# K and V in 256 KB transfers into rings freed per two heads, with at most 1.3 MB in flight

## The chip, the cores and the metric

One Trainium2 chip, one of its cores. The metric is the device time of one execution in microseconds (us), as a median of several runs. Traces were taken by the hardware profiler on one execution of each kernel. The engines are called by their names in the profile: PE is TensorE (PEld its weight loads), DVE VectorE, ACT ScalarE, POOL GpSimd, and SP SyncE, whose queue issues the loads. The granted clock is the share of full clock speed that PE was allowed; at half clock it is one half.

One run of the kernel before, 1038.62 us, was slow and is not compared. Kernels that were run only once, with a profile, have the state "unknown" and are used for their mechanism, not for their time to a per cent. The profiled execution of the kernel before took 1035.58 us, 1% more than its median.

## The reference

Two independent attention blocks, A and B, with a cached K and V; their outputs are concatenated.

```python
# B=16, Sq=64, D=640, H=32, Sk=512, Dh=128, all bfloat16; twice (A and B)
q      = (x @ wq).reshape(B, Sq, H, Dh).transpose(0, 2, 1, 3)
scores = einsum("bhqd,bhkd->bhqk", q, k_cache) * Dh**-0.5
p      = softmax(scores)
o      = einsum("bhqk,bhkd->bhqd", p, v_cache)
y      = o.transpose(0, 2, 1, 3).reshape(B, Sq, H*Dh) @ wo
```

K and V of both blocks are 268 MB; with the weights, and x once for each half of the heads, the kernels here read 294.65 MB.

## The kernel before

A static plan. For every pair of batches and every pair of heads, one *step* runs: PE transposes K (32 small matmuls), projects q (10), makes scores (4), transposes the probabilities (16), multiplies by V (16) and by wo (4). There are 256 steps. PE's whole program is unrolled, about 42,000 matmuls and weight loads.

All loads go through SP's queue, in an order that the plan fixes. K and V come in pieces of G heads of one batch:

```python
class Cfg:
    G = 4               # heads in one K or V transfer: 4 * 512 * 128 * 2 bytes = 512 KB
    NKB = 5; NVB = 5    # ring slots, each of G heads of two batches
    NXN = 1             # one buffer for x
    ...

# build_plan: the loads, with the step from which the slot is free and the step that needs it
    for c in range(NCHUNK):
        ...
        for kind, ring, n_ring, cons, tb in (("LDK", "kn", cfg.NKB, "KX", 2), ("LDV", "v", cfg.NVB, "PV", 2.5)):
            ready = NEG if c < n_ring else MPC * (c - n_ring + 1) - 1 - OFF[cons]
            need = MPC * c - OFF[cons]
            ...                                     # two transfers, one for each batch
# SP issues in order of need; a transfer waits only for the readers of its slot:
        op.deps = [d for d in deps if d is not op and not (d.eng == op.eng and op.eng in ("pe", "sp"))
                   and not (d.dma and op.dma and d.eng == op.eng)]
# the emitter
            src = blocks[blk][1][2 * bp + j, h0 + hlo:h0 + hhi].rearrange("(hp hs) (p t) d -> (hs p) hp t d", hs=2, t=8)
            ins = e.dma_start(kn_ring[:, c % NKB, j, hlo // 2:hhi // 2], src)
```

So the only limit on the bytes in flight is that a ring slot must be free.

Of the kernel before, what the change touches and what calls it, by code (L numbers as in the profile page):

```python
# [19 lines left out]


class Cfg:
    G = 4
    HH = 16
    NKB = 5
    NVB = 5
    NX = 3
    NXN = 1
    NQ = 2
# [24 lines left out]
        act=("EX0", "EX1", "XE0", "OE0", "OVP0", "ST0"),  # L54
        pool=("NM0", "NM1"),
    )
    TAIL_SPLIT = 2
    SLOT_NS = 3040.0
    DMA_NS = dict(LDK=1340.0, LDV=1460.0, LDWQ=1800.0, LDWO=1900.0, LDX=700.0)


class Op:
# [16 lines left out]
        self.dma = kind in DMA_KINDS  # L79


def build_plan(dims, cfg, stable):
    NBLK, B, H = dims["NBLK"], dims["B"], dims["H"]
    G = cfg.G
    HH = min(cfg.HH, H)
    assert H % HH == 0 and HH % G == 0 and G % 2 == 0 and cfg.NR % 2 == 0 and B % 2 == 0
    NHALF = H // HH
    assert NHALF in (1, 2)
    NBP = B // 2
    NPASS = NBLK * NHALF  # L90
    NGRP = NPASS * NBP
    NSTEP = NGRP * HH
    NMAC = NSTEP // 2
    NCHUNK = NSTEP // G
    HG = HH // G
    MPG = HH // 2
    MPP = NBP * MPG
    MPC = G // 2
    tag = "g" if stable else "f"

    OFF = {}
    for eng, kind, sub, off in cfg.PERIOD:
        OFF.setdefault(kind, off)
# [7 lines left out]
    def make_op(eng, kind, sub, k, m):  # L111
        ts = (k, STAGE[kind + str(sub)])

        def mk(idx, reads, writes, aux=None, name=None):
            return Op(eng, name or kind, idx, reads, writes, ts=ts, aux=aux)
# [11 lines left out]
        ps_, bp, grp, h0 = place(m)  # L127
        g0 = 2 * m
        g = g0 + sub
        c = g0 // G  # L130
        r = g % cfg.NR
# [2 lines left out]
        if kind == "KE":  # L134
            return mk((m, sub), [], [("KT", sub), ("ktp", m % cfg.NKT, sub)])
        if kind == "QP":
            return mk(m, [("xT", grp % cfg.NX), ("wq", ps_ % 2, h0 // G)], [("A",)])
        if kind == "QE":
            return mk(m, [], [("A",), ("qT", m % cfg.NQ)])
        if kind == "SM":  # L140
# [17 lines left out]
        if kind == "OE":  # L158
            return mk(m, [], [("B",), ("oT", m % cfg.NO)])
        if kind == "OP":  # L160
            return mk(m, [("oT", m % cfg.NO), ("wo", ps_ % 2, h0 // G)], [("OUT",)])
        if kind in ("OVP", "OVF", "ST"):
            if h0 + 2 != HH:
                return None
# [10 lines left out]
    progs = {e: [] for e in ENGINES}  # L175
    lo = -max(max(OFF.values()), cfg.XLEAD)
    for k in range(lo, NMAC):
        for eng, order in cfg.ENGINE_ORDER.items():
            for name in order:
                kind, sub = name[:-1], int(name[-1])  # L180
                op = make_op(eng, kind, sub, k, k + OFF[kind])
# [17 lines left out]
    loads = []  # L199
    NEG = -10 ** 9  # L200
    for ps_ in range(NPASS):
        buf = ps_ % 2
        for j in range(HG):
            m0 = ps_ * MPP + j * MPC
            for kind, name, cons, tb in (("LDWQ", "wq", "QP", 0), ("LDWO", "wo", "OP", 3)):
                ready = NEG if ps_ < 2 else (ps_ - 1) * MPP - MPG + j * MPC + MPC - 1 - OFF[cons]
                need = m0 - OFF[cons]
                op = Op("sp", kind, (ps_, j), [], [(name, buf, j)], ts=(need, -1), aux=(ps_, j),
                        dur=cfg.DMA_NS[kind] * G / 4.0)
                loads.append((ready, need, tb, op))  # L210
    for grp in range(NGRP):
        need = MPG * grp - cfg.XLEAD
        op = Op("sp", "LDX", grp, [], [("xn", grp % cfg.NXN)], ts=(need, STAGE["KX0"]), aux=grp,
                dur=cfg.DMA_NS["LDX"])
        loads.append((NEG if grp < cfg.NXN else need - MPG * cfg.NXN, need - 1, 1, op))
    for c in range(NCHUNK):
        n = cfg.TAIL_SPLIT if c == NCHUNK - 1 else 1
        w = G // n
        for kind, ring, n_ring, cons, tb in (("LDK", "kn", cfg.NKB, "KX", 2), ("LDV", "v", cfg.NVB, "PV", 2.5)):
            ready = NEG if c < n_ring else MPC * (c - n_ring + 1) - 1 - OFF[cons]  # L220
            need = MPC * c - OFF[cons]
            for i in range(n):
                for j in range(2):
                    op = Op("sp", kind, (c, j, i), [], [(ring, c % n_ring, gi) for gi in range(i * w, i * w + w, 2)],
                            ts=(need, -1), aux=(c, j, i * w, i * w + w, i), dur=cfg.DMA_NS[kind] * w / G)
                    loads.append((ready, need + 0.01 * i, tb + 0.001 * (2 * i + j), op))
    pending = sorted(loads, key=lambda e: (e[1], e[2]))
    t_now = min(e[1] for e in loads) - 4.0
    while pending:
        cand = [e for e in pending if e[0] <= t_now]  # L230
        if cand:
            e = cand[0]
        else:
            e = min(pending, key=lambda e_: (e_[0], e_[1], e_[2]))
# [2 lines left out]
        progs["sp"].append(e[3])  # L237
        t_now += e[3].dur / cfg.SLOT_NS

    counts = {}  # L240

    def sem_key(op):
        if op.kind in ("LDK", "LDV"):
            return (tag + "d_" + op.kind[2:].lower(), op.writes[0][1], op.aux[4])
        if op.kind == "LDX":
            return (tag + "d_x", op.writes[0][1])
        if op.kind in ("LDWQ", "LDWO"):
            return (tag + "d_" + op.kind[2:].lower(), op.aux[0] % 2, op.aux[1])
        if op.kind == "ST":
            return (tag + "d_out", op.aux % 2)  # L250
        if op.kind in ("INIT1", "INIT2"):
            return (tag + "s_init",)
        return (tag + "s_" + op.kind.lower(),)

    def assign(op):
        key = sem_key(op)
# [14 lines left out]
    for op in sorted(all_ops, key=lambda o: o.ts):  # L271
        deps = []
        for res in op.reads:
            w = last_writer.get(res)
# [3 lines left out]
        for res in op.writes:  # L278
            w = last_writer.get(res)
            if w is not None:  # L280
                deps.append(w)
            for rd in readers.get(res, ()):
                if rd is not op:
# [2 lines left out]
            readers[res] = []  # L286
        op.deps = [d for d in deps if d is not op and not (d.eng == op.eng and op.eng in ("pe", "sp"))
                   and not (d.dma and op.dma and d.eng == op.eng)]
    info = dict(NSTEP=NSTEP, NBP=NBP, HH=HH, NHALF=NHALF, counts=counts)
    return progs, info  # L290


# [51 lines left out]
def mha_kernel(nc, blocks, out, cfg=None):  # L344
    cfg = cfg or Cfg()
# [3 lines left out]
    _, H, SK, DH = k0.shape  # L349
    assert SQ == 64 and DH == 128 and SK == 512 and D % 128 == 0 and B % 2 == 0  # L350
    KT = D // 128
    G = cfg.G
    scale = float(DH) ** -0.5
    N0 = min(D, 512)
    N1 = D - N0
# [1 line left out]

    dims = dict(NBLK=NBLK, B=B, H=H)
    plans = []
    for stable in (False, True):  # L360
        progs, info = build_plan(dims, cfg, stable)
        prune_waits(progs)
        plans.append((progs, info))
    info = plans[0][1]
    NBP, HH, NHALF, NSTEP = info["NBP"], info["HH"], info["NHALF"], info["NSTEP"]
    NKB, NVB, NX, NXN, NQ, NKT, NP, NPN, NT, NO, NR = (cfg.NKB, cfg.NVB, cfg.NX, cfg.NXN, cfg.NQ, cfg.NKT, cfg.NP,
                                                       cfg.NPN, cfg.NT, cfg.NO, cfg.NR)
# [10 lines left out]
    with contextlib.ExitStack() as es:  # L378
# [5 lines left out]
        wq_sb = sb("wq_sb", [128, 2, KT, HH * DH], BF16)  # L384
        wo_sb = sb("wo_sb", [128, 2, HH, D], BF16)
# [3 lines left out]
        kn_ring = sb("kn_ring", [128, NKB, 2, G // 2, 8, DH], BF16)  # L389
        v_ring = sb("v_ring", [128, NVB, 2, G, 4, DH], BF16)  # L390
# [15 lines left out]
        ps = es.enter_context(nc.psum_tensor("ps", [128, 8, 512], F32))  # L406

        sems = {}
        for _, inf in plans:
            for key in sorted(inf["counts"].keys(), key=str):  # L410
                sems[key] = es.enter_context(nc.semaphore("_".join(str(k) for k in key)))

        out_ps0 = ps[:, 0, 0:N0]
        out_ps1 = ps[:, 1, 0:N1] if N1 > 0 else None
# [191 lines left out]
        def em_LDWQ(e, op):  # L606
            ps_, j = op.aux
            blk, half = ps_ // NHALF, ps_ % NHALF
            c0 = (half * HH + j * G) * DH
            src = blocks[blk][3].rearrange("(kt p) n -> p kt n", p=128)[:, :, c0:c0 + G * DH]  # L610
            ins = e.dma_start(wq_sb[:, ps_ % 2, :, j * G * DH:(j + 1) * G * DH], src)  # L611
            return ins, ins

        def em_LDWO(e, op):
            ps_, j = op.aux
            blk, half = ps_ // NHALF, ps_ % NHALF
            h0 = half * HH + j * G
            src = blocks[blk][4].rearrange("(h d) n -> d h n", d=DH)[:, h0:h0 + G, :]
            ins = e.dma_start(wo_sb[:, ps_ % 2, j * G:(j + 1) * G, :], src)
            return ins, ins  # L620

        def em_LDX(e, op):
# [15 lines left out]
            return ins, ins  # L638

        def em_LDKV(e, op):  # L640
            c, j, hlo, hhi, _piece = op.aux
            blk, bp, grp, ps_, hh0 = place(c * G // 2)
            h0 = (ps_ % NHALF) * HH + hh0
            if op.kind == "LDV":
                src = blocks[blk][2][2 * bp + j, h0 + hlo:h0 + hhi].rearrange("g (p t) d -> p g t d", p=128)
                ins = e.dma_start(v_ring[:, c % NVB, j, hlo:hhi], src)  # L646
            else:
                src = blocks[blk][1][2 * bp + j, h0 + hlo:h0 + hhi].rearrange("(hp hs) (p t) d -> (hs p) hp t d",
                                                                              hs=2, t=8)
                ins = e.dma_start(kn_ring[:, c % NKB, j, hlo // 2:hhi // 2], src)  # L650
            return ins, ins

        emitters = dict(KX=em_KX, KE=em_KE, QP=em_QP, QE=em_QE, SM=em_SM, MX=em_MX, MS=em_MS, RC=em_RC, NM=em_NM, TR=em_TR,
# [2 lines left out]
                        LDWO=em_LDWO, LDX=em_LDX, LDK=em_LDKV, LDV=em_LDKV)  # L656

        def step(key):
            return 16 if key[0][1:].startswith("d_") else 1

        def run_program(e, prog, stable):
            for op in prog:
# [9 lines left out]
                    first.wait_op(sems[s], v * step(s), "sem-ge")  # L672
                last.then_inc(sems[op.sem], 16 if op.dma else 1)

        stores = [[(k, v) for k, v in inf["counts"].items() if k[0].endswith("d_out")] for _, inf in plans]

        def wait_stores(e, which):
            for s, v in stores[which]:
# [2 lines left out]
        def run_engine(e, name):  # L681
            run_program(e, plans[0][0][name], False)
            if name == "act":
                wait_stores(e, 0)
            e.wait_ge(sems[("fs_cf",)], 1)
            redo = e.value_load(flag[0:1, 0:1])
            with e.If(redo > 0):
                if name == "sp":
                    wait_stores(e, 0)
                run_program(e, plans[1][0][name], True)  # L690
                if name == "act":
                    wait_stores(e, 1)
# [69 lines left out]
```

## Time and profile before

| | before |
|---|---|
| time, median of 3 runs (a fourth came with the result: 1025.69 us) | 1025.61 us (1024.35 to 1032.01) |
| PE busy | 837.1 us, 81% |
| DMA rate, mean; two best slices | 291; 365 and 366 GB/s |
| granted clock of PE | 0.952 |
| bytes in flight, mean and most (own count from issues and landings) | 2.1 and 4.6 MB |

Page of the kernel before, cut. Part 1 has busy time and share of the span; part 2 has 40 slices of the span with busy tenths, the granted PE clock in tenths, and what the DMA engines moved; part 3 a DMA queue with its packets, MB and share; part 4 the chain of work that ended last.

```profile
span 1033.8 us, 47133 instructions
...
PE 837.1 (81%) x20900; PEld 606.1 (59%) x21153; DVE 669.2 (65%) x1812; ACT 447.8 (43%) x1329; POOL 416.9 (40%) x518
...
PEclk9899999999998999999999999999989999989998
DMA  9999899999888899989988689998899878789840
GB/s 317 365 366 348 279 312 297 304 303 309 272 296 288 299 321 302 314 271 314 345 282 300 221 278 344 303 300 271 269 320 366 290 247 280 264 290 327 292 146 12
...
q8 instruction: 170, 2.79, 1.1%
...
PE 77%; issue 16%; DVE 4%; SPq 1%; DMA 1%; ACT 1%; ACTq 0%; DVEq 0%
```

No engine is full and the DMA rate is below its own best slices, yet the chain holds 16% "issue": PE was idle and waited for nothing that the profile names. The waits view of PE (who waited, for whom: us in total, times, longest) says that these are few and long:

```profile
PE ps L431 <- issue: 73.4, 53, 2.9
PE ps L535 <- issue: 36.5, 24, 2.3
PE ps L457 <- issue: 27.0, 14, 2.9
PE ps L631 <- DMA xn_ring<-in_A_x_dram: 12.4, 2, 9.2
```

One of them, in PE's timeline (start in us, duration, line and operation; idle time before it in brackets):

```profile
505.10 0.55 PE L431 MATMUL ps<-ident,kn_ring 64*128 64x64 bf16 x26
507.14 0.26 PE L431 MATMUL ps<-ident,kn_ring 64*128 64x64 bf16 x6 [1.49 <-issue]
```

PE stops in the middle of 32 like transposes, whose data is all there: 26, a gap of 1.49 us, the other 6. Such gaps lie at multiples of 254.5 recorded PE instructions. Queue q8, which the profile labels "instruction", has 170 packets of 16 KB, one for every 254.5 recorded PE instructions, and the gaps end 1.2 to 1.7 us after one of them has landed. I read them as PE waiting for its own program, of which one such packet brings a block. I call them *fetch pauses* and count them from the trace's records as follows: PE and its weight loads both idle for over 0.3 us, ended 1.0 to 1.8 us after an instruction packet, and no data or engine released just before.

K and V transfers, from issue to landing (median us at the end; two of four groups, 5.8 to 8.8 us in all):

```profile
kn_ring<-in_A_k_cache_dram SPq DMA_DIRECT2D x128, 512.0 KB, 6.8
v_ring<-in_B_v_cache_dram SPq DMA_DIRECT2D x126, 512.0 KB, 8.1
```

### The profile page before, as it was taken

To read this page: it belongs to the slowest core of one execution; us is meant where nothing else is said; L and a number is where in the kernel's file an instruction comes from. 1 tells how busy PE (TensorE), PEld (TensorE's weight loads), DVE (VectorE), ACT (ScalarE), POOL (GpSimd) and SP (SyncE) were. 2 spreads that over 40 slices of the span, in tenths; PEclk is the share of its full clock that TensorE was granted. 3 is DMA by queue.
4 is the path that set the end of the run, shared out by engine and by line. 5 is a ranking of instruction groups with operands and counts; after the bars stand their busy time and mean duration, and the time that the engine had idled before them with its cause. 6 is when DMAs were issued, how large, how long until landed. Compare 5 with 4: busy or idle time off the path is not lost.

```text
span 1033.8 us, 47133 instructions
## 1 busy us (share of the span) xinstructions
PE 837.1 (81%) x20900; PEld 606.1 (59%) x21153; DVE 669.2 (65%) x1812; ACT 447.8 (43%) x1329; POOL 416.9 (40%) x518
## 2 busy tenths in 40 slices
PE   3876879888788878888788888888788888888885
PEld 2555656656556656665565655665555656665664
DVE  1565667666666767676676666676656666666674
ACT  1343444444444444444444444444444444434442
POOL 0433444443443444444344343444434344344442
PEclk9899999999998999999999999999989999989998
DMA  9999899999888899989988689998899878789840
GB/s 317 365 366 348 279 312 297 304 303 309 272 296 288 299 321 302 314 271 314 345 282 300 221 278 344 303 300 271 269 320 366 290 247 280 264 290 327 292 146 12
DMA packets 230930, 300.42 MB, mean 291 GB/s; under 512 B 9536, under 2 KB 165184, under 8 KB 230720
## 3 DMA queue, kind: packets, MB, share of 16 engines
q1 hardware_dynamic: 228416, 294.69, 84.4%
q8 instruction: 170, 2.79, 1.1%
q10 hardware_dynamic: 2304, 2.62, 0.7%
q14 instruction: 40, 0.33, 0.1%
HBM read 294.65 MB, written 2.62 MB: 288 GB/s over the span
## 4 chain that ended last, share of the span: by engine, by line
PE 77%; issue 16%; DVE 4%; SPq 1%; DMA 1%; ACT 1%; ACTq 0%; DVEq 0%
PE ps L431 21%; PE ps L457 16%; PE ps L470 14%; PE ps L551 12%; PE ps L535 12%; DVE ktp_ring L447 2%; PE ps L631 1%; DMA xn_ring<-in_A_x_dram 1%; DVE pT_ring L522 1%; ACT p_ring L491 1%; DVE out_sb L564 0%; SPq L646 0%; SPq L650 0%; SPq L611 0%; DVE qT_ring L463 0%
## 5 line engine op out<-in xcount | busy, mean ns | idle before, releaser
L506 POOL TENSOR_SCALAR pn_ring<-p_ring,recip 128x512 bf16<-128x512 bf16 x512 | 416.2, 842 | 602.3 <-DVE recip L498 602.3
L447 DVE COPY ktp_ring<-ps 128x1024 bf16<-128x1024 bf16 x512 | 345.5, 681 | 200.7 <-PE ps L431 200.7
L491 ACT ACTIVATE p_ring<-ps 128x512 bf16<-128x512 f32 x512 | 301.1, 594 | 53.4 <-PE ps L470 24.0
L540 ACT ACTIVATE oT_ring<-ps 128x256 bf16<-128x256 f32 x256 | 98.1, 383 | 454.0 <-DVE pT_ring L522 452.8
L522 DVE COPY pT_ring<-ps 128x512 bf16<-128x512 bf16 x512 | 193.1, 419 | 129.3 <-PE ps L535 128.8
L431 PEld LDWEIGHTS ps<-ident,kn_ring 64*128 64x128 bf16 x8192 | 141.5, 97 | 147.0 <-issue 131.7
L457 PE MATMUL ps<-xT_ring,wq_sb 128*128 128x128 bf16 x2560 | 198.3, 226 | 31.0 <-issue 27.0
L535 PE MATMUL ps<-pT_ring,v_ring 128*128 128x64 bf16 x4096 | 174.2, 197 | 36.5 <-issue 36.5
L431 PE MATMUL ps<-ident,kn_ring 64*128 64x64 bf16 x8192 | 175.8, 194 | 32.8 <-issue 30.7
L535 PEld LDWEIGHTS ps<-pT_ring,v_ring 128*128 128x128 bf16 x4096 | 153.6, 101 | 42.2 <-issue 41.6
L457 PEld LDWEIGHTS ps<-xT_ring,wq_sb 128*128 128x128 bf16 x2560 | 150.7, 100 | 45.4 <-issue 27.8
L470 PE MATMUL ps<-ktp_ring,qT_ring 128*64 128x512 bf16 x1024 | 170.5, 411 | 7.5 <-issue 4.0
L551 PE MATMUL ps<-wo_sb,oT_ring 128*128 128x128 bf16 (+1 forms) x771 | 134.1, 285 | 21.2 <-issue 8.8
L431 PE MATMUL ps<-ident,pn_ring 64*128 64x64 bf16 x4096 | 108.9, 192 | 47.0 <-issue 42.6
L463 DVE CAST qT_ring<-ps 128x256 bf16<-128x256 f32 x256 | 108.5, 424 | 17.8 <-PE ps L457 9.2
L431 PEld LDWEIGHTS ps<-ident,pn_ring 64*128 64x128 bf16 x4096 | 81.7, 96 | 48.4 <-issue 44.1
L491 ACT ACTIVATION_READ_ACCUMULATOR p_ring<-ps 128x1 f32 x512 | 102.4, 200 | 0.0
L551 PEld LDWEIGHTS ps<-wo_sb,oT_ring 128*128 128x128 bf16 x1024 | 76.1, 101 | 39.8 <-issue 12.0
L470 PEld LDWEIGHTS ps<-ktp_ring,qT_ring 128*64 128x64 bf16 x1024 | 38.9, 110 | 83.5 <-issue 78.9
L498 DVE RECIPROCAL recip<-sums 128x1 f32<-128x1 f32 x512 | 78.5, 153 | 8.1 <-ACT p_ring L491 8.1
L636 ACT ACTIVATE xT_ring<-ps 128x640 bf16<-128x640 bf16 x32 | 22.5, 704 | 68.4 <-PE ps L631 68.4
L631 PE MATMUL ps<-ident,xn_ring 128*128 128x128 bf16 x160 | 15.1, 228 | 14.4 <-DMA xn_ring<-in_A_x_dram 12.4
(16 smaller groups left out, 39.5 us busy)
## 6 DMA issues: line engine op xcount, KB each, us to landing
kn_ring<-in_A_k_cache_dram SPq DMA_DIRECT2D x128, 512.0 KB, 6.8
v_ring<-in_A_v_cache_dram SPq DMA_DIRECT2D x128, 512.0 KB, 5.8
kn_ring<-in_B_k_cache_dram SPq DMA_DIRECT2D x126, 512.0 KB, 8.8
v_ring<-in_B_v_cache_dram SPq DMA_DIRECT2D x126, 512.0 KB, 8.1
wq_sb<-in_A_wq_dram SPq DMA_DIRECT2D x8, 640.0 KB, 10.4
wo_sb<-in_A_wo_dram SPq DMA_DIRECT2D x8, 640.0 KB, 9.5
wq_sb<-in_B_wq_dram SPq DMA_DIRECT2D x8, 640.0 KB, 9.3
wo_sb<-in_B_wo_dram SPq DMA_DIRECT2D x8, 640.0 KB, 9.6
```

The lines of the kernel that those rows point to most:

```text
L431: return e.transpose(dst, src, ident[rows(r), rows(r)], tile_position=(64 * r, 0))
L447: ins = e.tensor_copy(ktp_ring[:, m % NKT, hs].rearrange("p j k -> p (j k)"), kt_ps(hs))
L457: ins.append(e.matmul(q_ps[:, sub * 128:(sub + 1) * 128], wq_sb[:, ps_ % 2, kt, hh * DH:(hh + 1) * DH], xT_ring[:, grp % NX, kt, :], start ...
L463: ins = e.tensor_copy(qT_ring[:, op.idx % NQ].rearrange("p s q -> p (s q)"), q_ps)
L470: ins.append(e.matmul(ps[64 * j:64 * j + 64, S_BANK + sub, :], qT_ring[:, m % NQ, sub, 64 * j:64 * j + 64], ktp_ring[:, m % NKT, sub, j, : ...
L491: ins = e.activation(p_ring[:, g % NP, :], ps[:, S_BANK + g % 2, :], ACTF.Exp, scale=scale, accum_out=sums[:, g:g + 1], **kw)
L498: ins = e.reciprocal(recip[:, g % NR:g % NR + 1], sums[:, g:g + 1])
L506: ins = e.tensor_scalar(dst, src, recip[:, r:r + 1], 1.0, ALU.mult, ALU.mult)
L522: ins = e.tensor_copy(pT_ring[:, m % NT, j].rearrange("p s t q -> p (s t q)"), ps[:, A_BANK + j, 0:256].bitcast(BF16))
L535: ins.append(e.matmul(o_ps[:, col:col + 64], v_ring[:, c % NVB, j, gi, t, :], pT_ring[:, m % NT, j, sub, t, :], start=(t == 0), stop=(t == ...
L540: ins = e.activation(oT_ring[:, op.idx % NO].rearrange("p s q -> p (s q)"), o_ps, ACTF.Copy)
L551: ins.append(e.matmul(dst, oT_ring[:, m % NO, sub, :], wo_sb[:, ps_ % 2, hh, c0:c1], start=(hh == 0), stop=(hh == HH - 1)))
```

## The change

Halve the transfers, free ring slots twice as often, and let SP hold back a transfer until those in flight, with it, are at most 1.3 MB, so that fewer bytes of K and V are in flight when an instruction block is fetched: in the trace of before, the block's packet starts about 0.9 us plus 1.1 us per MB in flight after PE enters the block before. Weights keep their pieces of four heads (GW). The core of the diff:

```diff
 class Cfg:
-    G = 4
+    G = 2
+    GW = 4
+    CAP = 1300 << 10
-    NKB = 5
-    NVB = 5
+    NKB = 10
+    NVB = 10
@@ the loads: one K and one V transfer of G heads for each batch; the split of the last chunk goes @@
-        n = cfg.TAIL_SPLIT if c == NCHUNK - 1 else 1
...
+            for j in range(2):
+                op = Op("sp", kind, (c, j), [], [(ring, c % n_ring, gi) for gi in range(0, G, 2)],
+                        ts=(need, -1), aux=(c, j), dur=cfg.DMA_NS[kind] * G / 2.0)
@@ after the dependencies @@
+    size = dict(LDK=G << 17, LDV=G << 17, LDX=160 << 10, LDWQ=GW * 160 << 10, LDWO=GW * 160 << 10)
+    window = []
+    for op in progs["sp"]:
+        window.append(op)
+        done = None
+        while sum(size[o.kind] for o in window) > cfg.CAP:
+            done = window.pop(0)
+        if done is not None:
+            op.deps.append(done)
```

(Line edits that follow from these, and one set of semaphores shared by the two copies of the plan instead of two.) Five transfers of 256 KB fit into the window. Bytes, data packets and all compute instructions stay as they were: SP's queue moves 294.7 MB, with 8,128 more small packets, 16 for each of the 508 additional transfers. (PE has 20900 matmuls in one page and 21153 in the other because records are missing in the first, so the two PE busy times are not compared to a per cent.) In the profiles of the changed kernel the line numbers are 4 higher (L431 is L435).

More of the change, by code (lines that the diff above doesn't have):

```diff
@@ L56 @@
     )
-    TAIL_SPLIT = 2
     SLOT_NS = 3040.0
-    DMA_NS = dict(LDK=1340.0, LDV=1460.0, LDWQ=1800.0, LDWO=1900.0, LDX=700.0)
+    DMA_NS = dict(LDK=670.0, LDV=730.0, LDWQ=1800.0, LDWO=1900.0, LDX=700.0)
 class Op:
@@ L79, in __init__, with build_plan @@
         self.dma = kind in DMA_KINDS
-def build_plan(dims, cfg, stable):
+def build_plan(dims, cfg, stable, counts):
     NBLK, B, H = dims["NBLK"], dims["B"], dims["H"]
-    G = cfg.G
+    G, GW = cfg.G, cfg.GW
     HH = min(cfg.HH, H)
@@ L94, in build_plan @@
     NCHUNK = NSTEP // G
-    HG = HH // G
+    HG = HH // GW
     MPG = HH // 2
@@ L98, in build_plan @@
     MPC = G // 2
-    tag = "g" if stable else "f"
+    MPW = GW // 2
     OFF = {}
@@ L136, in make_op @@
         if kind == "QP":
-            return mk(m, [("xT", grp % cfg.NX), ("wq", ps_ % 2, h0 // G)], [("A",)])
+            return mk(m, [("xT", grp % cfg.NX), ("wq", ps_ % 2, h0 // GW)], [("A",)])
         if kind == "QE":
@@ L160, in make_op @@
         if kind == "OP":
-            return mk(m, [("oT", m % cfg.NO), ("wo", ps_ % 2, h0 // G)], [("OUT",)])
+            return mk(m, [("oT", m % cfg.NO), ("wo", ps_ % 2, h0 // GW)], [("OUT",)])
         if kind in ("OVP", "OVF", "ST"):
@@ L203, in build_plan @@
         for j in range(HG):
-            m0 = ps_ * MPP + j * MPC
+            m0 = ps_ * MPP + j * MPW
             for kind, name, cons, tb in (("LDWQ", "wq", "QP", 0), ("LDWO", "wo", "OP", 3)):
-                ready = NEG if ps_ < 2 else (ps_ - 1) * MPP - MPG + j * MPC + MPC - 1 - OFF[cons]
+                ready = NEG if ps_ < 2 else (ps_ - 1) * MPP - MPG + j * MPW + MPW - 1 - OFF[cons]
                 need = m0 - OFF[cons]
                 op = Op("sp", kind, (ps_, j), [], [(name, buf, j)], ts=(need, -1), aux=(ps_, j),
-                        dur=cfg.DMA_NS[kind] * G / 4.0)
+                        dur=cfg.DMA_NS[kind])
                 loads.append((ready, need, tb, op))
@@ L216, in build_plan @@
     for c in range(NCHUNK):
-        n = cfg.TAIL_SPLIT if c == NCHUNK - 1 else 1
-        w = G // n
         for kind, ring, n_ring, cons, tb in (("LDK", "kn", cfg.NKB, "KX", 2), ("LDV", "v", cfg.NVB, "PV", 2.5)):
@@ L221, in build_plan @@
             need = MPC * c - OFF[cons]
-            for i in range(n):
-                for j in range(2):
-                    op = Op("sp", kind, (c, j, i), [], [(ring, c % n_ring, gi) for gi in range(i * w, i * w + w, 2)],
-                            ts=(need, -1), aux=(c, j, i * w, i * w + w, i), dur=cfg.DMA_NS[kind] * w / G)
-                    loads.append((ready, need + 0.01 * i, tb + 0.001 * (2 * i + j), op))
+            for j in range(2):
+                op = Op("sp", kind, (c, j), [], [(ring, c % n_ring, gi) for gi in range(0, G, 2)],
+                        ts=(need, -1), aux=(c, j), dur=cfg.DMA_NS[kind] * G / 2.0)
+                loads.append((ready, need, tb + 0.001 * j, op))
     pending = sorted(loads, key=lambda e: (e[1], e[2]))
@@ L238, in build_plan @@
         t_now += e[3].dur / cfg.SLOT_NS
-    counts = {}
     def sem_key(op):
         if op.kind in ("LDK", "LDV"):
-            return (tag + "d_" + op.kind[2:].lower(), op.writes[0][1], op.aux[4])
+            return ("d_" + op.kind[2:].lower(), op.writes[0][1], op.aux[1])
         if op.kind == "LDX":
-            return (tag + "d_x", op.writes[0][1])
+            return ("d_x", op.writes[0][1])
         if op.kind in ("LDWQ", "LDWO"):
-            return (tag + "d_" + op.kind[2:].lower(), op.aux[0] % 2, op.aux[1])
+            return ("d_" + op.kind[2:].lower(), op.aux[0] % 2, op.aux[1])
         if op.kind == "ST":
-            return (tag + "d_out", op.aux % 2)
+            return ("d_out", op.aux % 2)
         if op.kind in ("INIT1", "INIT2"):
-            return (tag + "s_init",)
-        return (tag + "s_" + op.kind.lower(),)
+            return ("s_init",)
+        return ("s_" + op.kind.lower(),)
     def assign(op):
@@ L288, in build_plan @@
                    and not (d.dma and op.dma and d.eng == op.eng)]
-    info = dict(NSTEP=NSTEP, NBP=NBP, HH=HH, NHALF=NHALF, counts=counts)
+    size = dict(LDK=G << 17, LDV=G << 17, LDX=160 << 10, LDWQ=GW * 160 << 10, LDWO=GW * 160 << 10)
[7 more added lines that the diff above has]
+            op.deps.append(done)
+    info = dict(NSTEP=NSTEP, NBP=NBP, HH=HH, NHALF=NHALF, counts=dict(counts))
     return progs, info
@@ L351, in mha_kernel @@
     KT = D // 128
-    G = cfg.G
+    G, GW = cfg.G, cfg.GW
     scale = float(DH) ** -0.5
@@ L359, in mha_kernel @@
     plans = []
+    counts = {}
     for stable in (False, True):
-        progs, info = build_plan(dims, cfg, stable)
+        progs, info = build_plan(dims, cfg, stable, counts)
         prune_waits(progs)
@@ L408, in mha_kernel @@
         sems = {}
-        for _, inf in plans:
-            for key in sorted(inf["counts"].keys(), key=str):
-                sems[key] = es.enter_context(nc.semaphore("_".join(str(k) for k in key)))
+        for key in sorted(counts.keys(), key=str):
+            sems[key] = es.enter_context(nc.semaphore("_".join(str(k) for k in key)))
         out_ps0 = ps[:, 0, 0:N0]
@@ L608, in em_LDWQ @@
             blk, half = ps_ // NHALF, ps_ % NHALF
-            c0 = (half * HH + j * G) * DH
-            src = blocks[blk][3].rearrange("(kt p) n -> p kt n", p=128)[:, :, c0:c0 + G * DH]
-            ins = e.dma_start(wq_sb[:, ps_ % 2, :, j * G * DH:(j + 1) * G * DH], src)
+            c0 = (half * HH + j * GW) * DH
+            src = blocks[blk][3].rearrange("(kt p) n -> p kt n", p=128)[:, :, c0:c0 + GW * DH]
+            ins = e.dma_start(wq_sb[:, ps_ % 2, :, j * GW * DH:(j + 1) * GW * DH], src)
             return ins, ins
@@ L616, in em_LDWO @@
             blk, half = ps_ // NHALF, ps_ % NHALF
-            h0 = half * HH + j * G
-            src = blocks[blk][4].rearrange("(h d) n -> d h n", d=DH)[:, h0:h0 + G, :]
-            ins = e.dma_start(wo_sb[:, ps_ % 2, j * G:(j + 1) * G, :], src)
+            h0 = half * HH + j * GW
+            src = blocks[blk][4].rearrange("(h d) n -> d h n", d=DH)[:, h0:h0 + GW, :]
+            ins = e.dma_start(wo_sb[:, ps_ % 2, j * GW:(j + 1) * GW, :], src)
             return ins, ins
@@ L640, in em_LDKV @@
         def em_LDKV(e, op):
-            c, j, hlo, hhi, _piece = op.aux
+            c, j = op.aux
             blk, bp, grp, ps_, hh0 = place(c * G // 2)
@@ L644, in em_LDKV @@
             if op.kind == "LDV":
-                src = blocks[blk][2][2 * bp + j, h0 + hlo:h0 + hhi].rearrange("g (p t) d -> p g t d", p=128)
-                ins = e.dma_start(v_ring[:, c % NVB, j, hlo:hhi], src)
+                src = blocks[blk][2][2 * bp + j, h0:h0 + G].rearrange("g (p t) d -> p g t d", p=128)
+                ins = e.dma_start(v_ring[:, c % NVB, j], src)
             else:
-                src = blocks[blk][1][2 * bp + j, h0 + hlo:h0 + hhi].rearrange("(hp hs) (p t) d -> (hs p) hp t d",
+                src = blocks[blk][1][2 * bp + j, h0:h0 + G].rearrange("(hp hs) (p t) d -> (hs p) hp t d",
                                                                               hs=2, t=8)
-                ins = e.dma_start(kn_ring[:, c % NKB, j, hlo // 2:hhi // 2], src)
+                ins = e.dma_start(kn_ring[:, c % NKB, j], src)
             return ins, ins
@@ L658, in step @@
         def step(key):
-            return 16 if key[0][1:].startswith("d_") else 1
+            return 16 if key[0].startswith("d_") else 1
         def run_program(e, prog, stable):
@@ L673, in run_program @@
                 last.then_inc(sems[op.sem], 16 if op.dma else 1)
-        stores = [[(k, v) for k, v in inf["counts"].items() if k[0].endswith("d_out")] for _, inf in plans]
+        stores = [[(k, v) for k, v in inf["counts"].items() if k[0] == "d_out"] for _, inf in plans]
         def wait_stores(e, which):
@@ L684, in run_engine @@
                 wait_stores(e, 0)
-            e.wait_ge(sems[("fs_cf",)], 1)
+            e.wait_ge(sems[("s_cf",)], 1)
             redo = e.value_load(flag[0:1, 0:1])
```

## The prediction

> **What bounds the kernel now.** Neither engine work nor bandwidth, but a stall of the TensorE. The page shows PE busy 837 us of 1033.8, DVE 669, and DMA engines 84% occupied at a mean 291 GB/s, while slices two and three reach 365 and 366 GB/s. One step (two heads of two batches), measured from the first K transpose of one step to that of the next in the trace, takes 3.03 us wherever nothing disturbs it; 256 of them are 777 us. The median is 3.33 us and a quarter take over 4.5 us. In the chain of waits 16% of the span (about 168 us) is "issue": PE waits for nothing that the profile names. Those pauses last 0.4 to 3 us and sit at multiples of 254.5 recorded PE instructions. [...]the instruction queue moved 170 packets of 16 KB, and every such pause ends 1.3 to 1.6 us after one of them lands. [...]here I count 94 pauses, 150 us. [...]it starts about 0.9 us plus 1.1 us per MB in flight after PE enters the block before (fitted over 152 blocks), takes 1.07 us itself, and in-flight bytes average 2.1 MB, up to 4.6. That makes 5 to 7 us against about 4.7 us in which PE uses up a block.
>
> The pauses also cost clock: the granted clock halves for some 89 us, nearly always just after one, which lengthens the steps by about 40 us.
>
> **What the change does.** Bytes, descriptor sizes and all compute instructions stay. 508 transfers of 512 KB (and 8 of 256) become 1024 of 256 KB; ring capacity is equal, but a slot is freed after two heads instead of four. No transfer is issued if it would bring over 1.3 MB into flight: typically five K or V transfers. SP issues 1088 transfers rather than 580; at the 0.49 us median of the 256 KB ones that is about 530 us, which fits beside the other work. By the fit, at 1.1 to 1.3 MB a fetch starts after 2.1 to 2.4 us and is usable at about 4.7: the long pauses vanish, short ones (mean 0.2 to 0.4 us a block) remain, an estimate of 30 to 60 us in place of 150. The clock loss falls to 10 to 15 us. Start-up also gains a few us: the second x transfer took 8 us to land behind 3 MB.
>
> **Limit on the gain.** PE alone would then need about 777 + 18 (x transposes) + 35 (ends) = 830 us. The DMA becomes equally tight: 294.7 MB at 366 GB/s is 805 us plus the ends, about 825. The window costs some rate: 256 KB lands in about 2.8 us at best, so five keep the engines fed on average[...]. I expect 335 to 350 GB/s in the middle, which is 842 to 880 us. Both limits and residual pauses together: **885 us**, 80% range 850 to 935. Faster by over 2%: 0.94; within 2%: 0.05; slower: 0.01.
>
> **Checks.** Right if "issue" falls from 16% of the chain to under 7%, K and V land in 3 to 4.5 us, mean rate rises to 325 to 345 GB/s, the clock to about 0.98, and PE's waits turn partly into waits for K or V.
>
> **What would make it wrong.** The window starves the DMA (rate under 310 GB/s: time over 930); the fetch's delay comes not from bytes in flight, so pauses stay; or SP's issue time grows with the waits.

The sum came to 885 us. The 335 to 350 GB/s, and the 842 to 880 us and 885 us that rest on it, are estimates from the measured 366 GB/s. In "it starts about 0.9 us", "it" is the packet of an instruction block. The 2.8 us are close to what the trace of before shows: its one 256 KB transfer with nothing else in flight landed after 2.73 us.

## The result and the profile after

1080.61 us (median of 4 runs, 1077.29 to 1086.83) against 1025.69 us (median of 4): slower by 5.3%, ratio 1.053 with a 95% interval of 1.046 to 1.060. (A ratio is the mean time of one kernel's fast runs over that of the other's in the same rounds, so not quite the ratio of the medians quoted.)

The page of the changed kernel, the same parts:

```profile
span 1075.6 us, 48286 instructions
...
PE 863.2 (80%) x21153; PEld 605.5 (56%) x21153; DVE 671.6 (62%) x1812; ACT 447.5 (42%) x1329; POOL 416.0 (39%) x518
...
PEclk7979899988999999999987999999997889999998
DMA  7888888889888999988878898999878789899994
GB/s 232 266 260 278 270 281 282 294 278 303 274 261 287 307 301 304 290 287 286 283 256 266 274 303 277 285 302 311 287 257 254 238 297 305 299 299 295 301 305 140
...
q8 instruction: 170, 2.79, 1.1%
...
DMA 92%; SPq 3%; PE 3%; issue 1%; DVE 0%; ACT 0%; DVEq 0%
```

The bound has moved. "Issue" fell from 16% to 1% of the chain: the fetch pauses are gone. In its place 92% of the chain is DMA, although no slice reaches even 315 GB/s, where the kernel before had moved 366. PE's waits are nearly all for data now:

```profile
PE ps L635 <- DMA xn_ring<-in_A_x_dram: 68.1, 14, 15.7
PE ps L435 <- DMA kn_ring<-in_B_k_cache_dram: 38.1, 34, 4.5
PE ps L539 <- DMA v_ring<-in_B_v_cache_dram: 31.5, 49, 1.7
PE ps L555 <- DMA wo_sb<-in_B_wo_dram: 16.4, 8, 3.5
...
PE ps L461 <- issue: 3.3, 5, 1.4
```

A stretch of PE's timeline: its longest waits are for x, which stands in SP's order behind the window.

```profile
504.38 0.64 PE L539 MATMUL ps<-pT_ring,v_ring 128*128 128x64 bf16 x16 [0.54 <-DMA v_ring<-in_A_v_cache_dram]
511.04 0.69 PE L635 MATMUL ps<-ident,xn_ring 128*128 128x128 bf16 x5 [6.01 <-DMA xn_ring<-in_B_x_dram]
511.52 1.27 PE L555 MATMUL ps<-wo_sb,oT_ring 128*128 128x512 bf16 x4
512.72 1.06 PE L474 MATMUL ps<-ktp_ring,qT_ring 128*64 128x512 bf16 x4
...
516.62 0.62 PE L474 MATMUL ps<-ktp_ring,qT_ring 128*64 128x512 bf16 x4
```

After that wait the four matmuls of L474 take 1.06 us; one step later they take 0.62. That is the halved clock: the trace grants half from 507.9 to 514.7 us. Transfers are half as large as before, but take more than half the time to land:

```profile
kn_ring<-in_A_k_cache_dram SPq DMA_DIRECT2D x256, 256.0 KB, 4.4
v_ring<-in_B_v_cache_dram SPq DMA_DIRECT2D x256, 256.0 KB, 4.4
```

By own count in both traces (from 25 us to 15 us before the end): pauses of PE over 0.15 us 154 us before, of which 147 are fetch pauses; 173 us after, of which 169 are waits for data and 4 fetch pauses. Time at half clock went from 89 to 140 us. Steps that touch such time are longer than the undisturbed 3.034 us, pauses left out, by about 40 us before and 51 us after. These two differences (+19 and +11) and the 5 us that the start and the end take longer make 35 of the +42 us of the two spans; the count does not place the rest.

### The profile page after: what moved, and what is told of

Same layout as the page of the kernel before. It is cut to its first block, busy times and chain, and to the rows that moved or that the text cites. A ratio compares the mean times of both kernels' runs of the same rounds, so it can differ in the third digit from the quotient of the medians.

```text
span 1075.6 us, 48286 instructions
## 1 busy us (share of the span) xinstructions
PE 863.2 (80%) x21153; PEld 605.5 (56%) x21153; DVE 671.6 (62%) x1812; ACT 447.5 (42%) x1329; POOL 416.0 (39%) x518
## 2 busy tenths in 40 slices
DMA packets 239065, 300.51 MB, mean 279 GB/s; under 512 B 17664, under 2 KB 173312, under 8 KB 238848
## 4 chain that ended last, share of the span: by engine, by line
DMA 92%; SPq 3%; PE 3%; issue 1%; DVE 0%; ACT 0%; DVEq 0%
DMA kn_ring<-in_B_k_cache_dram 22%; DMA kn_ring<-in_A_k_cache_dram 21%; DMA v_ring<-in_B_v_cache_dram 20%; DMA v_ring<-in_A_v_cache_dram 16%; DMA wq_sb<-in_B_wq_dram 3%; DMA wo_sb<-in_A_wo_dram 3%; DMA xn_ring<-in_A_x_dram 3%; DMA wo_sb<-in_B_wo_dram 2%; SPq L650 2%; DMA wq_sb<-in_A_wq_dram 2%; SPq L654 1%; PE ps L555 1%; PE ps L435 1%; PE ps L539 1%; PE ps L474 0%
## 5 line engine op out<-in xcount | busy, mean ns | idle before, releaser
L435 PEld LDWEIGHTS ps<-ident,kn_ring 64*128 64x128 bf16 x8192 | 142.1, 98 | 161.5 <-DMA kn_ring<-in_B_k_cache_dram 74.3
L435 PE MATMUL ps<-ident,kn_ring 64*128 64x64 bf16 x8192 | 173.0, 195 | 47.3 <-DMA kn_ring<-in_B_k_cache_dram 38.1
L539 PE MATMUL ps<-pT_ring,v_ring 128*128 128x64 bf16 x4096 | 168.2, 196 | 48.3 <-DMA v_ring<-in_B_v_cache_dram 31.5
L555 PE MATMUL ps<-wo_sb,oT_ring 128*128 128x512 bf16 (+1 forms) x1024 | 190.3, 310 | 20.1 <-DMA wo_sb<-in_B_wo_dram 16.4
L539 PEld LDWEIGHTS ps<-pT_ring,v_ring 128*128 128x128 bf16 x4096 | 145.1, 100 | 64.8 <-DMA v_ring<-in_B_v_cache_dram 41.9
L474 PE MATMUL ps<-ktp_ring,qT_ring 128*64 128x512 bf16 x1024 | 168.9, 409 | 0.7
L435 PE MATMUL ps<-ident,pn_ring 64*128 64x64 bf16 x4096 | 107.2, 194 | 5.9 <-ACT oT_ring L544 2.7
L435 PEld LDWEIGHTS ps<-ident,pn_ring 64*128 64x128 bf16 x4096 | 82.2, 98 | 8.6 <-issue 5.2
L474 PEld LDWEIGHTS ps<-ktp_ring,qT_ring 128*64 128x64 bf16 x1024 | 37.9, 110 | 74.0 <-issue 70.7
```

The lines of the kernel that those rows point to most:

```text
L435: return e.transpose(dst, src, ident[rows(r), rows(r)], tile_position=(64 * r, 0))
L474: ins.append(e.matmul(ps[64 * j:64 * j + 64, S_BANK + sub, :], qT_ring[:, m % NQ, sub, 64 * j:64 * j + 64], ktp_ring[:, m % NKT, sub, j, : ...
L539: ins.append(e.matmul(o_ps[:, col:col + 64], v_ring[:, c % NVB, j, gi, t, :], pT_ring[:, m % NT, j, sub, t, :], start=(t == 0), stop=(t == ...
L555: ins.append(e.matmul(dst, oT_ring[:, m % NO, sub, :], wo_sb[:, ps_ % 2, hh, c0:c1], start=(hh == 0), stop=(hh == HH - 1)))
```

## The experiments

Theory A: the 1.3 MB window cannot keep the 16 DMA engines (the profile's count) fed, so the DMA rate sets the time; the pauses that it removes are real and depend on the bytes in flight. Rival B: 256 KB transfers are themselves slower (twice the issues and completions). Rival C: the pauses are PE's own and do not come from data traffic. Rival D: the loss is x arriving late behind the window. The runs below are in the order in which they were made; each table or number comes from the profiled run, each time from four runs, unless it says otherwise. The timed runs came in sets, each with its own runs of the kernel before (medians 1025.69 to 1027.93 us), so kernels of two sets are best compared by their ratios to it.

### The window taken away: `nocap`

```diff
-    CAP = 1300 << 10
+    CAP = 65536 << 10
```

> The change without its window (256 KB transfers, rings freed per two heads, no cap). Theory A, the 1.3 MB window starves the DMA: the rings alone now limit, bytes in flight go to 2 to 4.6 MB, K and V land in 6 to 9 us, the fetch pauses of PE come back (120 to 160 us against about 4 with the window), the waits for data (about 170 us) go, and the time is 1000 to 1035 us, as before the change. Theory B, 256 KB transfers are themselves slower (twice the transfers, issues and completions): the chain stays on DMA, the rate stays at or under 290 GB/s, and the time is 1060 us or more.

Measured: 1004.13 us, ratio to before 0.977 (0.972 to 0.981). Landing 7.1 us, mean in flight 2.0 MB, 129 us of fetch pauses, no waits for data. Rival B has fallen: the smaller transfers, with rings freed per two heads, make the kernel 2.3% *faster* than before (1.9 to 2.8%; so faster, but not clearly by 2%). The whole loss is the window's: against `nocap` the change is 7.6% slower by the medians of their two sets of runs.

### Other windows: `cap1600`, `cap2100`, `cap2900`, then `cap1850`, `cap2360`

```diff
-    CAP = 1300 << 10
+    CAP = 1600 << 10      # six transfers; 1850: seven, 2100: eight, 2360: nine, 2900: eleven
```

> Window of six 256 KB transfers instead of five. Theory A: the rate follows the window, 6/5 of 281 GB/s is up to about 325 GB/s as long as the landing time stays near 4.4 to 4.8 us; waits for data fall from 170 us to 40 to 90; fetch pauses stay under 30 us; time 950 to 1010 us. Theory B: within 2% of the change (1060 to 1100).

> Window of eight transfers. Theory A: the DMA is no longer starved (waits for data under 40 us, landing 5 to 6 us), fetch pauses come back in part (by the fit of the kernel before, fetch usable after about 5.5 us against 4.7 of work: 40 to 100 us); time 890 to 970 us, the best of the series or next to it. Theory B: within 2% of the change.

> Window of eleven transfers. Theory A: no waits for data, fetch pauses of 80 to 140 us, time 940 to 1010 us, between that of eight transfers and that without a window. Theory B: within 2% of the change.

> Window of seven 256 KB transfers. Theory A: the stream alone does 282 GB/s with five transfers and 354 with eight, so about 330 to 345 with seven; data waits of 10 to 50 us left, fetch pauses 50 to 80 us; time 950 to 980 us, within 2% of the window of eight.

> Window of nine. Theory A: no data waits, fetch pauses 95 to 115 us; time 955 to 985 us, so the best window is seven or eight.

| kernel | 256 KB transfers in the window | mean MB in flight | landing, us | GB/s, 100 to 600 us | fetch pauses, us | waits for data, us | half clock, us | time, us |
|---|---|---|---|---|---|---|---|---|
| the change | 5 | 1.21 | 4.4 | 283 | 4 | 169 | 140 | 1081 |
| cap1600 | 6 | 1.45 | 4.8 | 308 | 32 | 79 | 68 | 996 |
| cap1850 | 7 | 1.67 | 5.2 | 333 | 75 | 6 | 31 | 940 |
| cap2100 | 8 | 1.73 | 5.6 | 333 | 92 | 2 | 17 | 958 |
| cap2360 | 9 | 1.75 | 6.1 | 316 | 123 | 0 | 58 | 985 |
| cap2900 | 11 | 1.91 | 6.9 | 309 | 123 | 0 | 78 | 1001 |
| nocap | no limit | 2.00 | 7.1 | 309 | 129 | 0 | 65 | 1004 |
| before (512 KB) | no limit | 2.11 | 7.2 | 297 | 147 | 0 | 89 | 1026 |

Two opposite curves. Fewer bytes in flight give fewer fetch pauses and more waits for data, and the time has a minimum where the second has just ended: seven transfers, 940.17 us, ratio 0.917 (0.911 to 0.923) to before. With nine and more, the rate falls because PE is slow again, not because the DMA is: a stream that does not wait for PE reaches 360 and 366 GB/s (`free2100` and `free4600` below). The times expected of theory A held, with these misses: seven transfers did better than their 950 to 980 us, with fewer waits for data (6 us for 10 to 50), and beat eight by 1.9% (another set; the intervals of the ratios, 0.911 to 0.923 and 0.926 to 0.941, do not overlap); nine had more pauses than expected (123 us for 95 to 115) and just missed its upper edge; six had 32 us of pauses for under 30, and 308 GB/s for up to 325.

The chains of `cap1600`, `cap1850` and `nocap`, in this order, show the bound moving back from the DMA to PE and its fetch pauses:

```profile
DMA 66%; PE 23%; DVE 3%; SPq 3%; issue 3%; ACT 1%; ACTq 0%; DVEq 0%
PE 78%; issue 10%; DMA 5%; DVE 5%; ACT 1%; ACTq 0%; SPq 0%; DVEq 0%
PE 78%; issue 15%; DVE 4%; SPq 1%; DMA 1%; ACT 1%; ACTq 0%; DVEq 0%
```

In `cap1850` all of the 5% DMA lies in the first 54 us; after the start no data transfer is on its chain.

### PE and the stream measured apart: `pe_alone`, `free1300`, `free2100`, `free4600`

Their outputs are wrong, which doesn't matter for the times. PE reads the same two K and V chunks, the same x and two passes' weights again and again; in the `free` kernels all other K and V chunks are streamed into slots that nobody reads, held back by the window alone (here every transfer that leaves the window is waited for, so that the reuse of a slot is ordered). Only the main lines of the edit:

```diff
-            return mk(m, [("kn", c % cfg.NKB, g0 % G), ("ident",)], ...
+            return mk(m, [("kn", c % cfg.NST, g0 % G), ("ident",)], ...   # NST = 2
-    for c in range(NCHUNK):
+    for c in range(NCHUNK if cfg.STREAM else cfg.NST):
-            ready = NEG if c < n_ring else MPC * (c - n_ring + 1) - 1 - OFF[cons]
+            ready = NEG
+            slot = c if c < cfg.NST else cfg.NST + (c - cfg.NST) % (n_ring - cfg.NST)
-            done = window.pop(0)
+            op.deps.append(window.pop(0))
```

> Wrong result on purpose. All compute instructions of the change, but K, V, x are loaded once (two heads' worth of chunks, one x) and read again and again, weights loaded for two passes only: after the start no data moves. Theory A (PE pauses come from instruction blocks fetched behind K and V): no pauses over 0.3 us at the multiples of a block, step time 3.03 us, clock over 0.98, time 800 to 850 us. Rival C (the pauses are PE's own, every block boundary costs them): about 150 us of pauses and 950 us or more.

> Wrong result on purpose. As the kernel without traffic, but all K and V chunks are also streamed into buffers that nobody reads, with the 1.3 MB window and no other wait: DMA rate and PE pauses each for itself. Theory A: the stream runs at 270 to 300 GB/s although nothing but the window holds it (so the starving is the window's own), PE has pauses of under 20 us in all. Theory B (PE or the ring waits held the stream in the change): 340 GB/s or more.

> As the one before with a window of eight transfers (2.1 MB). Theory A: 340 to 365 GB/s, PE pauses of 0.2 to 0.6 us a block while the stream runs. Theory B: the same rate as with 1.3 MB.

> As the one before with a window of 4.6 MB. Theory A: 360 to 370 GB/s, hardly more than with 2.1 MB, but fetches wait longest: pauses of 1.5 to 4 us at nearly every block while the stream runs. Rival C: the pauses are the same in all four.

`pe_alone` took 824.04 us in its one run. Its page:

```profile
span 822.2 us, 46548 instructions
...
PE 784.0 (95%) x20900; PEld 575.8 (70%) x21153; DVE 664.9 (81%) x1812; ACT 446.3 (54%) x1329; POOL 417.0 (51%) x518
```

The same compute instructions and the same block boundaries (170 packets of q8), no pause at any of them after the start ("issue" is 1.4 us of PE's waits in all), no half clock after it (granted clock 1.00 from 100 to 600 us). Rival C has fallen: without data traffic the fetch cost no pause, and PE alone needed 822 us.

The stretch from 100 to 600 us of three kernels. The columns are the stretch, its length, busy us (and instructions) of PE, PEld, DVE, ACT and POOL, the granted PE clock, the DMA engines' mean busy share (over 1 where packets overlap) and GB/s of all queues. First `free1300`:

```profile
100.00:600.00 500.00, 436.74 (x11265) 320.34 (x11401) 358.76 (x976) 240.32 (x717) 224.50 (x277) 0.95 0.89 288
```

Then `free2100`:

```profile
100.00:600.00 500.00, 422.64 (x10881) 306.73 (x11014) 347.62 (x941) 232.56 (x692) 215.99 (x268) 0.98 1.05 360
```

Then `free4600`:

```profile
100.00:600.00 500.00, 383.77 (x9442) 276.44 (x9553) 303.13 (x819) 201.69 (x601) 187.35 (x232) 0.94 1.07 366
```

With five in flight and nothing else in its way the stream does 288 GB/s, of which SP's queue (K, V and weights) 282; in the change the same two figures are 283 and 277. So it is the window's own limit. Eight give 360; 17 are allowed in `free4600`, of which 11 or 12 were in flight for 88% of the time (about 3 MB; SP's issue then takes longer, 0.58 us in the median for 0.38), and give 366. PE's fetch pauses in the same stretches, per block (one packet of q8): 0 without a stream, about 0.1 us with five (8.4 us of "issue" in 90 blocks), 0.8 us with eight (over the 0.2 to 0.6 expected), 1.5 us with about 3 MB in flight (the lower end of the 1.5 to 4 expected). From eight to about twelve the rate hardly grows (360 to 366 GB/s) and the pauses nearly double (0.8 to 1.5 us): here they follow the bytes in flight, not the rate. The long waits of `free1300` are for weights at the start of the second pass (23 us for wq), not for instructions; with them PE's pauses are over the 20 us expected, and they make it a poorer measure of PE than the others.

### The window alone, at a better size: `g4_cap2100`

```diff
-    G = 2
-    CAP = 1300 << 10
-    NKB = 10
-    NVB = 10
+    G = 4
+    CAP = 2100 << 10
+    NKB = 5
+    NVB = 5
```

> The window alone, sized well: 512 KB transfers and rings freed per four heads as before the change, with a window of 2.1 MB, four transfers. If bytes in flight are what counts, the fetch pauses are those of eight 256 KB transfers (80 to 110 us) and the time is within 2.5% of it (940 to 985 us). If the finer transfers are what makes the window work (a window of few large pieces drains and refills unevenly), the rate is 20 GB/s lower or more, data waits of over 50 us appear and the time is 985 to 1020 us.

Measured: 984.32 us, ratio to before 0.960 (0.954 to 0.967); 319 GB/s, landing 5.9 us, 105 us of fetch pauses, 6 us of waits for data. It is 2.7% slower than eight transfers of 256 KB, just outside the expected 2.5%; the data waits that the other reading asked for did not come. So four 512 KB transfers in flight do most of what eight of 256 KB do: it is mainly the bytes in flight that count. The rest (13 us more pauses, 51 us at half clock for 17) belongs to the coarser pieces; why is not settled.

### x issued earlier: `x_early`

```diff
-    NXN = 1
+    NXN = 2
-        loads.append((NEG if grp < cfg.NXN else need - MPG * cfg.NXN, need - 1, 1, op))
+        loads.append((NEG if grp < 1 else need - MPG, need - 1, 1, op))
+    for i in [n for n, o in enumerate(progs["sp"]) if o.kind == "LDX"]:
+        progs["sp"].insert(max(i - 12, 0), progs["sp"].pop(i))
```

> The change with its 1.3 MB window, but every x transfer issued twelve transfers earlier, into a second x buffer. Theory A (the rate is short): the 57 us of waits for x turn into waits for K, V and wo, the rate stays at 280 to 290 GB/s and the time at 1060 to 1085 us. Rival D (x comes late because it queues behind the window, and that is what costs): the waits go, and the time falls by their 57 us and part of the half-clock time that follows the long ones, to 1000 to 1030 us.

Measured: 1083.69 us, against 1080.61 of the change. The waits for x have turned into waits for K and V (here L437 and L541 are the K transposes and the product with V):

```profile
PE ps L437 <- DMA kn_ring<-in_A_k_cache_dram: 55.7, 38, 4.4
PE ps L437 <- DMA kn_ring<-in_B_k_cache_dram: 44.4, 38, 5.2
PE ps L541 <- DMA v_ring<-in_A_v_cache_dram: 33.0, 49, 2.0
PE ps L541 <- DMA v_ring<-in_B_v_cache_dram: 28.1, 50, 1.9
```

The rate is 279 GB/s. Rival D has fallen: the largest single line of PE's waits was only the place where the shortage of bandwidth showed.

### What a transfer's landing time consists of: `free_w1`, `free_w3`

As `free1300`, with one and three transfers in flight (a guard keeps a 640 KB weight transfer from waiting for itself):

```diff
-        while sum(size[o.kind] for o in window) > cfg.CAP:
+        while len(window) > 1 and sum(size[o.kind] for o in window) > cfg.CAP:
-    CAP = 1300 << 10
+    CAP = 300 << 10       # free_w3: 800 << 10
```

> Wrong result on purpose: the free stream of K and V with one 256 KB transfer in flight, to measure the term that the prediction mis-sized (it took 2.8 us as the least landing time of 256 KB and concluded that five keep the engines fed). If the landing time is mostly a fixed latency: 2.9 to 3.4 us even alone, rate under 90 GB/s, and five in flight (4.4 us) are only about 1.4 times that. If it is mostly a queue behind the other four: 2.0 to 2.5 us alone, rate 100 GB/s or more. No pauses of PE while it runs.

> The same with three in flight. Fixed latency: 3.3 to 3.8 us, 200 to 235 GB/s, so the rate still grows with the window from three to five almost in proportion (282 with five). Queue: 2.8 to 3.1 us, 250 to 280 GB/s, as much as with five.

Medians of the 256 KB transfers issued between 100 and 600 us. Each transfer's semaphore gets 16 increments (9,536 for 596 transfers in the trace of before, 17,664 for 1,104 in that of the change), and the trace has the time of every one. I read each as the landing of a part of the transfer; the trace does not say what makes it:

| in flight | GB/s | first increment, us after issue | 8th increment | 16th increment |
|---|---|---|---|---|
| 1 | 98 | 2.21 | 2.37 | 2.64 |
| 3 | 219 | 2.36 | 2.59 | 3.40 |
| 5 | 288 | 2.70 | 3.20 | 4.46 |
| 8 | 360 | 3.48 | 4.26 | 5.70 |
| 11 or 12 (`free4600`) | 366 | 3.81 | 4.95 | 8.22 |

Neither expectation for one transfer was met: 2.64 us and 98 GB/s lie between them, and PE, though free of fetch pauses, was busy for only 172 of the 500 us: it stood still for weights (one wait of 405 us). With three, the rate (219) and landing (3.40 us) are those expected of a fixed latency. The table shows why both readings were too simple. A transfer alone needs 2.6 us, of which 2.2 pass before its first increment. With five in flight the first still comes after 2.7 us, but the last only after 4.5: the spread of the 16 grows from 0.4 to 1.7 us (2.3 with eight, 4.5 with about twelve; medians). The window opens on the last increment: in the change SP issued a transfer 0.02 us (median, own count) after the last increment of an earlier one. By count of the packets under way between 100 and 600 us, fewer than 16 are moving during 54% of the time in the change, 31% in `cap1850`, and 9% in `free2100`, and the mean busy share of the 16 DMA engines there is 0.88, 0.99 and 1.05. Fewer than 16 packets leave at least one of 16 engines without one; so in the change, by this estimate, some engine is often idle while others still work. With eight in flight the last increment comes after 5.7 us, and 8 x 262,144 bytes in 5.7 us are 368 GB/s; 360 were measured.

Which engines are idle, and whether they are the ones that were done early with a transfer, was not shown: the trace does not name the engine of a packet. The direct test, opening the window on 12 of 16 increments, was not run.

### Both together: `x_early_1850`

The edit of `x_early` with `CAP = 1850 << 10`.

> A candidate that should beat both: the window of seven transfers, and each x transfer twelve places earlier into a second buffer. The start should lose its wait for the second x transfer (PE's second step at about 13 us instead of 25), the pauses stay at 70 to 85 us; time 925 to 940 us against 940 for the window of seven alone.

Measured: 940.76 us, a touch over the expected 925 to 940, ratio to before 0.920 (0.913 to 0.927), the same as `cap1850`. The second step does start at 12.7 instead of 24.9 us, but by the twentieth the lead is down to 4 us (86.2 and 90.3), and the end gains nothing: 78 us of fetch pauses and 10 of waits for data in place of 75 and 6. Half of the lead goes in the first 54 us, where PE now waits for wo, K and V instead of x and the chain is still DMA: here an earlier start only brought the wait for data forward.

## Why the prediction was wrong

- **The bound before.** Right. PE stalled for its own instructions; `pe_alone` shows that the stalls vanish with the traffic (none, for 147 us of fetch pauses before), and the two series show that they grow with the bytes in flight (4 us at 1.21 MB to 129 at 2.00, and 0.1 to 1.5 us a block). PE's own limit was right too: 830 us predicted, 822 in `pe_alone`.
- **What the window does to the pauses.** Right in kind, and cautious in size: 4 us remain (30 to 60 predicted). In the free stream with the same window about 0.1 us a block remain, against 0.2 to 0.4 predicted.
- **The step that failed**: "The window costs some rate: 256 KB lands in about 2.8 us at best, so five keep the engines fed on average[...]. I expect 335 to 350 GB/s in the middle". The best landing time was right (2.6 us alone, `free_w1`). Wrong was to take the window over it (5 x 262,144 bytes in 2.8 us would be 468 GB/s, more than enough). With five in flight the landing time is 4.4 us, and 5 x 262,144 bytes in 4.4 us are 298 GB/s at the very most; 283 were measured. The prediction charges the window 4 to 8% of the rate, an estimate; it cost 23% (283 for 366 GB/s). The trace of before had a hint: the 16 increments of its 512 KB transfers are spread over 1.5 us in the median. So had the prediction's own checks: it allowed a landing time of 4.5 us, but five in flight give 335 GB/s only if they land within 3.9. Landing (4.4 us) and "issue" (1%) passed their checks, rate (279 in the mean) and clock failed.
- **PE's and the DMA's limits together.** 885 us rested on 335 to 350 GB/s. `cap1850` reaches 333 and takes 940: even where the rate is nearly as predicted, 75 us of fetch pauses come back with it. In none of the windows tried were both costs low together, and the prediction summed the best of each.
- **Clock.** Predicted to recover (10 to 15 us lost); it fell, 0.952 to 0.931. In the trace of before, all 25 stretches of half clock that began between the first 25 and the last 15 us did so during a pause of PE or within 2 us of its end; the longest such pause was 2.1 us in the median and never under 1.6 us. (Not every pause did this: 28 of the 53 over 1.6 us were followed by half clock within 9 us.) After the change it is again 25 stretches, but of up to 13.7 us for 6.8, and the pauses are 1.7 to 13.4 us, 3.0 in the median; 169 of the 173 us of pauses are waits for data. The traces show this order, not the cause. With seven and eight transfers it did recover: 31 and 17 us at half clock.
- **Start-up.** Predicted to gain a few us; the second step starts at 27.2 instead of 23.8 us, since x also queues for the window: PE waits 15.7 us for the second x transfer instead of 9.2.
- **SP's issue time.** Right: SP spends 480 us issuing (530 estimated), and `nocap`, where it is 640 us, is not held by it.
- The prediction named its own failure, "the window starves the DMA (rate under 310 GB/s: time over 930)", and gave it too little weight. It was within reach of paper: bytes in flight over landing time, at the landing time that holds *with* those bytes in flight.

## What to carry to other kernels

A long unrolled program lost time to its own data traffic (147 us of fetch pauses with 2.1 MB in flight in the mean, none in `pe_alone`): gaps labelled "issue", at equal distances in instructions (254.5 recorded) and 1.2 to 1.7 us after a 16 KB instruction packet, were read as waits for instruction fetches, and a limit on the bytes in flight shortened them (75 us at seven transfers, 4 at five). Here such a limit paid most at seven transfers (0.917 of the time before), little at six or eleven (0.967 and 0.972, where no limit gives 0.977), and cost time at five (1.053); its size had to cover the landing time of a transfer's *last* increment under load (five at 4.4 us gave 283 GB/s, seven at 5.2 us 333). In another kernel, sweep it, and watch the two curves, pauses and data waits, cross. When a limit has been set too tight, the largest wait in the list can tell where the shortage shows, not what causes it, as x did here.
